# An operand schedule written as a table: the seven-product scheme of an attention, soft-mixture and squared-ReLU kernel

## The chip, the cores and the metric

One core of a Trainium2 chip runs one program. The metric is device time in microseconds (us) of one execution; the profile of one execution and the times of three are shown below. The five engines that compute are called by the names of the profile: PE (matrix products), DVE (VectorE), ACT (ScalarE), POOL (GpSimd); SP issues transfers.

## The reference

Three layers follow each other. Attention over 768 positions with a local window, eight global positions and a linear distance penalty; a soft mixture of experts (every slot a weighted mean of all 3072 tokens, eight small two-layer networks on the slots, every token a weighted mean of the slots); and a last network with squared ReLU. Only the last is touched here:

```python
def _moe2_ref(x, w_in, w_out):
    h = x @ w_in                 # 3072 x 512 times 512 x 2048
    r = np.maximum(h, 0.0)
    g = r * r
    return (g @ w_out).astype(np.float32)
```

Since x itself is a product of token weights (32 slots) and slot outputs, the kernel forms `U = slot_out @ w_in` once and computes `h` as token weights times U, one matmul for 128 columns of `w_in` and 512 tokens.

## The kernel before

**Stages.** From some 225 us on the kernel runs the last network. The 2048 hidden units are cut in five parts q of 256, 384, 384, 512 and 512 (`WIDTHS`), the tokens in six chunks d of 512. For q = 0 to 3 and each d, `gemm1(q, d, j)` makes 128 hidden units: a product h on PE, a ReLU on ACT (line 1049), then `g` as a high part on ACT (1054) and a rest on POOL (1055), for which DVE (1053) or ACT has computed the square in full precision. `gemm2(q, d, m)` multiplies with 128 output columns m: for each j two products with the high part of g (`whi`, `wlo`) and one with its rest, 12 matmuls for four j. An eviction follows: a copy where q = 0 (line 1093, DVE for m = 3 and else ACT), an addition on DVE into `oacc` (1095) for the other q.

**The main loop** (lines 1322 to 1341) takes for each (q, d) four steps m. Below, the steps of q = 3 are numbered k = 4d + m, from 0 to 23. One step advances the generator `background` (the next part's weights: integers are turned into floats on ACT and DVE, U is formed, the weights are split in high part and rest), then issues `gemm1` one chunk ahead, then `gemm2`. At m = 0 only the products with the high part are issued; their rests follow at m = 1. Engines work in the order of issue, each on its own, and wait for each other by semaphores.

**The last part, q = 4,** has 512 units and is computed by a scheme with seven products in place of eight. Units and output columns are halved, and two chunks of tokens (a, b) form a pair p; there are three pairs. The seven left operands are made of weights: blocks x11, x12, x21, x22 and the differences s1 = x21 + x22, s2 = s1 - x11, s4 = x12 - s2, s3 = x11 - x21 (`conv_last`, 983 to 1015). The seven right operands are made of squared-ReLU blocks y11, y12, y22, y21 and t1 = y12 - y11, t2 = y22 - t1, t3 = y22 - y12, t4 = y21 - t2 (`y_make`, 1151 to 1174). Each operand is split in a high part (ACT, 994, 1129, 1131) and a rest, that is operand minus high part (POOL at 996; POOL or DVE at 1132). Two products h (1140) and two ReLUs (1141) and a square (1143) precede each y block. The y blocks and differences share four regions of one buffer: t2 takes y11's place, t3 takes t1's, y21 takes y12's, t4 takes y22's.

`pair` (1176) runs 14 groups g of six matmuls, P1, P5, P6, P3, P7, P2, P4 with two output halves each (lines 1200, 1201, 1203); each group ends with an addition on DVE (1183). After every second group the generator `y_make` is advanced by one operand, which issues all of that operand's operations, from products to rest, in a row. Operands of the next pair begin at g = 6. The first pair's are issued in the last four steps of the main loop.

**Scratch that is shared.** The PSUM tags `h` and `k` have two buffers each; `gemm1` takes them in turn, the products for y always take `h`. The tag `e` (1062, 1136) has two buffers, used by ReLU results of `gemm1` and of y. A buffer is given again only when all who read it are done.

Of the kernel before, what the change touches and what calls it, by code (L numbers as in the profile page):

```python
# [7 lines left out]
F32 = mybir.dt.float32  # L8
# [3 lines left out]
AF = mybir.ActivationFunctionType  # L12
ALU = mybir.AluOpType
# [7 lines left out]
P = 128  # L21
# [9 lines left out]
TB = 256  # L31
WIDTHS = [256, 384, 384, 512, 512]
# [8 lines left out]
def attention_moe_ffn(ctx: ExitStack, tc, qk, vx, nn, phi, w1, w2, w_in, w_out, consts, relw, out):  # L41
# [909 lines left out]
    def conv_in(q):  # L951
        W = WIDTHS[q]
        if q:
            t = slot("p4", [P, 4096], F32, f"winf{q}")
            f = t[:, 0 : 4 * W]
            if q == QL:
                raw["f"] = t[:, 4 * W : 8 * W].rearrange("p (j c) -> p j c", c=DM)
        else:
            f = hZ[:, E * HS : E * HS + 4 * W]
        wq[q] = {"f": f.rearrange("p (a c) -> p a c", c=W)}  # L960
        for c0 in range(0, 4 * W, 512):
            yield from convert(raw[q][0], c0, f[:, c0 : c0 + 512], f"i{q}")
            yield
# [19 lines left out]
    def conv_last():  # L983

        wf = raw["f"]
        for j in range(4):
            yield from convert(raw[QL][1], j * DM, wf[:, j, :], f"o{QL}")
            yield
        t = [slot(tag, [P, 4, 2, 2, 2 * P], F32R, f"x{tag}") for tag in ("s1", "p8")]
        x11, x12, x21, x22 = (wf[:, j : j + 2, c : c + 2 * P] for c, j in ((0, 0), (0, 2), (2 * P, 0), (2 * P, 2)))  # L990

        def operand(n, name, x):
            hi, lo = (t[n // 4][:, n % 4, a] for a in range(2))
            nc.scalar.copy(hi, x)
            yield
            G.tensor_tensor(lo, x, hi.bitcast(F32), op=ALU.subtract)
            xop[name] = hi, lo
            yield

        def diff(name, a, b, op=ALU.subtract):  # L1000
            x = ex.tile([P, 2, 2 * P], F32, tag="cvx", name=name, bufs=2)
            V.tensor_tensor(x, a, b, op=op)  # L1002
            return x

        yield from operand(0, "P1", x11)
        s1 = diff("xs1", x21, x22, ALU.add)
        yield from operand(1, "P5", s1)
        s2 = diff("xs2", s1, x11)
        yield from operand(2, "P6", s2)
        s4 = diff("xs4", x12, s2)  # L1010
        yield from operand(3, "P3", s4)
        s3 = diff("xs3", x11, x21)
        yield from operand(4, "P7", s3)
        yield from operand(5, "P2", x12)
        yield from operand(6, "P4", x22)

    def make_u(q):
        W = WIDTHS[q]
# [66 lines left out]
    def gemm2_lo(pa, q, d, m):  # L1085
        glo, whi = g_of(q, d)[:, 1, :, :], wq[q]["hi"]
        ms = slice(m * P, m * P + P)
        J = WIDTHS[q] // P
        for j in range(J):
            nc.tensor.matmul(pa, lhsT=whi[:, j, ms], rhs=glo[:, j, :], start=False, stop=j == J - 1)  # L1090
        o = oacc[d][:, m, :]
        if q == 0:
            (V.tensor_copy if m == 3 else nc.scalar.copy)(o, pa)
        else:
            V.tensor_tensor(o, pa, o, op=ALU.add)  # L1095

# [26 lines left out]
        t = yt[n - n % 2]  # L1123
        return t[:, n % 2, 0], t[:, n % 2, 1]

    def y_split(name, y, r, eng):
        hi, lo = y_parts(name)
        if r is None:
            nc.scalar.copy(hi, y)  # L1129
        else:  # L1130
            nc.scalar.activation(hi, r, AF.Square)
        eng.tensor_tensor(lo, y, hi.bitcast(F32), op=ALU.subtract)  # L1132
        yop[name] = hi, lo

    def y_block(name, k, half, chunk):
        r = ex.tile([P, 2, 2 * TB], F32, tag="e", name=f"r{name}_{chunk}", bufs=2)
        for jj in range(2):
            j = 2 * half + jj
            ph = fps.tile([P, 2 * TB], F32, tag="h", name=f"h{name}_{chunk}_{jj}", bufs=2)
            nc.tensor.matmul(ph, lhsT=wq[QL]["U"][:, j * P : j * P + P], rhs=cst[:, chunk * 2 * TB : chunk * 2 * TB + 2 * TB], start=True, stop=True)  # L1140
            nc.scalar.activation(r[:, jj], ph, AF.Relu)  # L1141
        y = region(name, k)
        nc.scalar.activation(y, r, AF.Square)  # L1143
        return y, r

    def y_diff(name, k, a, b):
        y = region(name, k)
        V.tensor_tensor(y, a, b, op=ALU.subtract)  # L1148
        return y

    def y_make(p):
        a, b = 2 * p, 2 * p + 1
        y11, r = y_block("y11", 0, 0, a)
        y_split("P1", y11, r, G)
        yield
        y12, _ = y_block("y12", 1, 0, b)
        t1 = y_diff("t1", 2, y12, y11)
        y_split("P5", t1, None, V)
        yield
        y22, r = y_block("y22", 3, 1, b)  # L1160
        t2 = y_diff("t2", 0, y22, t1)
        y_split("P6", t2, None, G)
        yield
        y_split("P3", y22, r, G)
        yield
        t3 = y_diff("t3", 2, y22, y12)
        y_split("P7", t3, None, V)
        yield
        y21, r = y_block("y21", 1, 1, a)
        y_split("P2", y21, r, G)  # L1170
        yield
        t4 = y_diff("t4", 3, y21, t2)
        y_split("P4", t4, None, G)
        yield

    def pair(p, make):
        a, b = 2 * p, 2 * p + 1
        A, Bk = {}, {}

        def add(pa, half, chunk, db, cs, done, eng):  # L1180
            m = 2 * half + db
            o = oacc[chunk][:, m, cs]
            V.tensor_tensor(o, pa[:, cs], o, op=ALU.add)
            if done:
                eng.dma_start(out[m * P : m * P + P, chunk * 2 * TB + cs.start : chunk * 2 * TB + cs.stop], o)

        def group(name, db, cs=slice(0, 2 * TB), n=0):
            if name in ("P1", "P6", "P7", "P4"):
                bank_, key, tag, nb = A, db, "acc", 3
            else:  # L1190
                bank_, key, tag, nb = Bk, (db, name == "P2", n), "k", 2
            new = key not in bank_
            if new:
                bank_[key] = fps.tile([P, 512], F32, tag=tag, name=f"b{p}{name}{db}{n}", bufs=nb)
            pa = bank_[key]
            (whi, wlo), (yhi, ylo) = xop[name], yop[name]
            c = slice(db * P, db * P + P)
            grown = {} if new else {"skip_group_check": True}
            for j in range(2):
                nc.tensor.matmul(pa[:, cs], lhsT=whi[:, j, c], rhs=yhi[:, j, cs], start=new and j == 0, stop=False, **grown)  # L1200
                nc.tensor.matmul(pa[:, cs], lhsT=wlo[:, j, c], rhs=yhi[:, j, cs], start=False, stop=False, **grown)  # L1201
            for j in range(2):
                nc.tensor.matmul(pa[:, cs], lhsT=whi[:, j, c], rhs=ylo[:, j, cs], start=False, stop=j == 1, **grown)
            half, chunk, done = {"P1": (0, a, False), "P5": (1, b, False), "P6": (0, b, False), "P3": (0, b, True),
                                 "P7": (1, b, True), "P2": (0, a, True), "P4": (1, a, True)}[name]
            add(pa, half, chunk, db, cs, done, nc.scalar if n else nc.sync)

        names = [(n, db) for n in ("P1", "P5", "P6", "P3", "P7") for db in range(2)]
        last = p == ND // 2 - 1
        names += [("P2", 0), ("P4", 0), ("P4", 1), ("P2", 1)] if last else [("P2", 0), ("P2", 1), ("P4", 0), ("P4", 1)]  # L1210
        for g, (n, db) in enumerate(names):
            if last and g == len(names) - 1:
                for c in range(2):
                    group(n, db, slice(c * TB, c * TB + TB), c)
            else:
                group(n, db)
            if g % 2 == 0:
                if g == 6:
                    make = y_make(p + 1) if not last else iter(())
                next(make, None)  # L1220
        return make

    def gemm2_first():
        whi, wlo = wq[0]["hi"], wq[0]["lo"]
# [92 lines left out]
            yield from c  # L1317

    ahead = [(q, d) for q in range(QL) for d in range(ND)][1:] + [None]
    make = y_make(0)  # L1320
    first_products = gemm2_first()
    for i in range(QL * ND):
        q, d = i // ND, i % ND
        if d == 0:
            bg = background(q + 1)
            total, room = 5 * (WIDTHS[q + 1] // P) + (17 if q + 1 == QL else 7), 4 * (ND - 1) - 1
        for m in range(4):
            k = 4 * d + m
            for _ in range((k + 1) * total // room - k * total // room):
                next(bg, None)  # L1330
            if d == ND - 1:
                for _ in bg:
                    pass
            if ahead[i]:
                gemm1(*ahead[i], m)
            else:
                next(make)
            if i:
                gemm2(q, d, m)
            else:  # L1340
                next(first_products, None)
    for p in range(ND // 2):
        make = pair(p, make)
    fps.release()
    stream.release()

# [160 lines left out]
```

## Time and profile before

| | us |
|---|---|
| three executions | 522.85, 525.3, 525.71 (median 525.3) |
| the profiled execution, its own time | 523.02 |
| its span (first to last instruction) | 521.2 |
| PE, share of the span with a matmul shown | 97% |
| main loop, q = 3 | some 338 to 446 |
| the three pairs | some 446 to 518 |

The profile lists each instruction with its line, engine, operation, operands and duration. A matmul's end is modelled: matmuls that follow each other are shown overlapping. The idle time in brackets is what the engine stood before that instruction, with the line that released it.

### The profile page before, as it was taken

To read this page: it belongs to the slowest core of one execution; us is meant where nothing else is said; L and a number is where in the kernel's file an instruction comes from. 1 tells how busy PE (TensorE), PEld (TensorE's weight loads), DVE (VectorE), ACT (ScalarE), POOL (GpSimd) and SP (SyncE) were. 2 spreads that over 40 slices of the span, in tenths; PEclk is the share of its full clock that TensorE was granted. 3 is DMA by queue.
4 is the path that set the end of the run, shared out by engine and by line. 5 is a ranking of instruction groups with operands and counts; after the bars stand their busy time and mean duration, and the time that the engine had idled before them with its cause. 6 is when DMAs were issued, how large, how long until landed. Compare 5 with 4: busy or idle time off the path is not lost.

```text
span 521.2 us, 9797 instructions
## 1 busy us (share of the span) xinstructions
PE 504.9 (97%) x3517; PEld 384.2 (74%) x3517; DVE 389.5 (75%) x922; ACT 334.1 (64%) x835; POOL 155.8 (30%) x119
## 2 busy tenths in 40 slices
PE   9999999999999999999999999999999979989897
PEld 6777777677777734588787888788878868768676
DVE  7788878887878747698685738687889853868685
ACT  6977878788788203488865766566646366574740
POOL 7000000000000110001553654476443783546352
PEclk9999999999999999999999999999999999998999
DMA  8789989999994899811312130404000000012224
GB/s 277 254 281 301 374 295 321 334 326 307 309 324 135 292 390 419 347 55 69 121 43 119 21 141 3 161 1 161 1 0 2 0 1 1 1 62 101 84 78 161
DMA packets 25975, 86.93 MB, mean 167 GB/s; under 512 B 2882, under 2 KB 5442, under 8 KB 23746
## 3 DMA queue, kind: packets, MB, share of 16 engines
q1 hardware_dynamic: 25776, 86.13, 46.4%
q8 instruction: 29, 0.48, 0.4%
q14 instruction: 24, 0.20, 0.1%
q10 hardware_dynamic: 146, 0.13, 0.1%
HBM read 79.95 MB, written 6.29 MB: 165 GB/s over the span
## 4 chain that ended last, share of the span: by engine, by line
PE 43%; DVE 11%; ACT 7%; issue 1%; POOL 0%; ACTq 0%; DVEq 0%
PE acc L1081 9%; PE acc L1090 9%; PE acc L1082 9%; PE pSO L923 3%; DVE yt L1148 3%; PE h L1061 2%; ACT yop L1129 1%; ACT ry L1141 1%; DVE yop L1132 1%; ACT yt L1143 1%; DVE xs L1002 1%; PE b2P L1200 1%; DVE oacc_p L1095 1%; PE b2P L1201 1%; ACT rg L1049 1%
## 5 line engine op out<-in xcount | busy, mean ns | idle before, releaser
L1081 PE MATMUL acc<-g,w 128*128 128x512 f32 x280 | 109.5, 391 | 3.8 <-ACT g L1054 2.8
L1082 PE MATMUL acc<-g,w 128*128 128x512 f32 x280 | 109.0, 389 | 0.0
L1055 POOL TENSOR_TENSOR g<-rg,g 128x512 fp32r<-128x512 f32 x60 | 81.3, 1361 | 77.1 <-DVE rg L1053 28.5
L263 ACT ACTIVATE sm<-sm,nm 128x256 f32<-128x256 f32 (+1 forms) x192 | 92.7, 488 | 1.6 <-DVE nm L248 1.6
L1090 PE MATMUL acc<-g,w 128*128 128x512 f32 x280 | 75.8, 390 | 0.0
L248 DVE CUSTOM_DVE_ANT_0 sm<-s,mask 128x256 f32<-128x256 f32 (+1 forms) x192 | 66.8, 397 | 2.0 <-ACT sm L263 1.2
L1049 ACT ACTIVATE rg<-h 128x512 f32<-128x512 f32 (+1 forms) x73 | 43.0, 589 | 38.9 <-PE h L1061 29.2
L1081 PEld LDWEIGHTS acc<-g,w 128*128 128x128 f32 x280 | 52.6, 188 | 16.0 <-ACT g L1054 3.2
L1090 PEld LDWEIGHTS acc<-g,w 128*128 128x128 f32 x280 | 52.5, 188 | 11.3 <-POOL g L1055 0.3
L1082 PEld LDWEIGHTS acc<-g,w 128*128 128x128 f32 x280 | 52.6, 188 | 10.8
L235 PE MATMUL s<-raw 64*128 64x256 f32 (+1 forms) x384 | 52.9, 397 | 0.0
L1132 POOL TENSOR_TENSOR yop<-yt,yop 128x1024 fp32r<-128x1024 f32 x15 | 37.9, 2533 | 42.0 <-ACT yop L1129 20.6
L1095 DVE TENSOR_TENSOR oacc_p<-acc,oacc_p 128x512 f32<-128x512 f32 x48 | 32.4, 687 | 23.3 <-PE acc L1090 23.3
L673 POOL TENSOR_TENSOR lh<-lh 128x256 f32<-128x256 f32 x1 | 0.7, 727 | 158.6 <-PE pt L274 158.6
L274 PE MATMUL pt<-con,sm 128*128 128x128 f32 x352 | 45.7, 278 | 1.6 <-ACT pT L280 1.6
L1054 ACT ACTIVATE g<-rg 128x512 fp32r<-128x512 f32 (+1 forms) x73 | 45.4, 622 | 1.6
L291 PE MATMUL o<-pT,v 128*64 128x128 f32 x704 | 44.2, 276 | 0.0
L274 PEld LDWEIGHTS pt<-con,sm 128*128 128x128 f32 x352 | 38.8, 141 | 7.3 <-ACT pT L280 2.8
L291 PEld LDWEIGHTS o<-pT,v 128*64 128x64 f32 x704 | 37.9, 137 | 6.9 <-ACT sm L263 2.1
L235 PEld LDWEIGHTS s<-raw 64*128 64x128 f32 x384 | 32.2, 194 | 14.6 <-DMA v<-in_vx 6.5
L1053 DVE SCALAR_TENSOR_TENSOR rg<-h,rg 128x512 f32<-128x512 f32 (+1 forms) x49 | 33.0, 675 | 10.0 <-ACT rg L1049 10.0
L263 ACT ACTIVATION_READ_ACCUMULATOR sm<-sm,nm 128x1 f32 x192 | 37.1, 193 | 0.0
(291 smaller groups left out, 874.2 us busy)
## 6 DMA issues: line engine op xcount, KB each, us to landing
w<-in_w SPq DMA_DIRECT2D x40, 512.0 KB, 6.4
raw<-in_qk SPq DMA_DIRECT2D x32, 384.0 KB, 5.0
w<-in_w SPq DMA_DIRECT2D x5, 2048.0 KB, 10.0
v<-in_vx SPq DMA_DIRECT2D x32, 256.0 KB, 4.3
raw<-in_qk SPq DMA_DIRECT2D x16, 320.0 KB, 4.9
win<-in_w_in SPq DMA_DIRECT2D x2, 2048.0 KB, 8.0
wout<-in_w_out SPq DMA_DIRECT2D x2, 2048.0 KB, 8.0
out_x<-oacc_p SPq DMA_DIRECT2D x15, 256.0 KB, 2.1
```

The costliest lines, as they stand in the source:

```text
L235: nc.tensor.matmul(sc[hh][:, tt, 0:n, :], lhsT=r[r0 : r0 + D, tt, :], rhs=rhs, start=True, stop=True)
L248: V.tensor_tensor_reduce(out=sm[:, j, 0:n, :], in0=sc[hh][:, tt, 0:n, :], in1=m[:, 2:3, :] if n == 1 else m[:, 0:2, :], scale=-QK_SCALE, s ...
L263: nc.scalar.activation(sm[:, j, 0:n, :], sm[:, j, 0:n, :], AF.Exp, bias=nm[:, j : j + 1], scale=-1.0, accum_out=chunk_sums(i // NPR)[:, tt ...
L274: nc.tensor.transpose(pp[tt][:, hh, c, :], sm[:, 2 * tt + hh, c, :], ident)
L291: nc.tensor.matmul(o[hh * D : hh * D + D, tt, :], lhsT=v[:, c * 3 if tt == 0 else 1 + c, hh * D : hh * D + D], rhs=pT[:, 2 * tt + hh, c, : ...
L1049: nc.scalar.activation(r, ph, AF.Relu)
L1054: nc.scalar.activation(g2[:, 0, js, cs], r, AF.Square)
L1055: (G if q else V).tensor_tensor(g2[:, 1, js, cs], g, g2[:, 0, js, cs].bitcast(F32), op=ALU.subtract)
L1081: nc.tensor.matmul(pa, lhsT=whi[:, j, ms], rhs=ghi[:, j, :], start=j == 0, stop=False)
L1082: nc.tensor.matmul(pa, lhsT=wlo[:, j, ms], rhs=ghi[:, j, :], start=False, stop=False)
L1090: nc.tensor.matmul(pa, lhsT=whi[:, j, ms], rhs=glo[:, j, :], start=False, stop=j == J - 1)
L1132: eng.tensor_tensor(lo, y, hi.bitcast(F32), op=ALU.subtract)
```

## The change

The generators `operand`, `diff`, `y_split`, `y_block`, `y_diff` and `y_make` go. In their place `y_steps(p)` puts each single operation (products, ReLUs, square, difference, high part, rest) into a numbered slot; slot n >= 0 stands behind group n of its own pair, and slots -14 to -1 stand behind the groups of the pair before (n + 14), or in the last steps of the main loop, two slots to a step, from k = 18. `make(p, slot)` issues what stands in a slot. A rest on POOL is issued as two instructions of half the size. The weight differences get buffers of their own (in the first half of the buffer whose second half holds the weights), all four are issued on DVE at the first two steps of `conv_last`, and `conv_last` takes 8 steps, not 14; it is to be done at k = 17. The eviction for q = 0 is on ACT for every m.

```diff
             if q == QL:
+                raw["s"] = t[:, 0 : 4 * W].rearrange("p (n j c) -> p n j c", n=4, c=2 * P)
                 raw["f"] = t[:, 4 * W : 8 * W].rearrange("p (j c) -> p j c", c=DM)
...
+        s1, s2, s3, s4 = (raw["s"][:, n] for n in range(4))
+        order = [("P1", x11), ("P5", s1), ("P6", s2), ("P3", s4), ("P7", s3), ("P2", x12), ("P4", x22)]
+        diffs = [(s1, x21, x22, ALU.add), (s2, s1, x11, ALU.subtract), (s4, x12, s2, ALU.subtract), (s3, x11, x21, ALU.subtract)]
+        for n in range(len(order) + 1):
+            if n < len(order):
+                name, x = order[n]
+                hi, lo = xop[name] = [t[n // 4][:, n % 4, a] for a in range(2)]
+                nc.scalar.copy(hi, x)
+            for o, x, y, op in diffs[2 * n : 2 * n + 2]:
+                V.tensor_tensor(o, x, y, op=op)
+            if n:
+                name, x = order[n - 1]
+                hi, lo = xop[name]
+                G.tensor_tensor(lo, x, hi.bitcast(F32), op=ALU.subtract)
             yield
...
-            (V.tensor_copy if m == 3 else nc.scalar.copy)(o, pa)
+            nc.scalar.copy(o, pa)
...
+        def low(name, y, eng):
+            hi, lo = y_parts(name)
+            for c in ((0, 1), (1, 2)) if eng is G else ((0, 2),):
+                c = slice(*c)
+                eng.tensor_tensor(lo[:, c], yt[y][:, c], hi[:, c].bitcast(F32), op=ALU.subtract)
+            yop[name] = hi, lo
...
+        for y, half, chunk, slot_ in (("y11", 0, a, -12), ("y12", 0, b, -10), ("y22", 1, b, -8), ("y21", 1, a, -3)):
+            step(slot_, products, y, half, chunk)
+            step(slot_ + 1, relu, y)
+        for y, k, slot_ in (("y11", 0, -10), ("y12", 1, -8), ("y22", 3, -6), ("y21", 1, 0)):
+            step(slot_, square, y, k)
...
+            step(slot_, diff, y, k, x0, x1)
...
+            step(s0, high, name, y)
+            step(s1, low, name, y, eng)
+        return at
...
+    def make(p, slot_):
+        for n in (p, p + 1):
+            if n < ND // 2:
+                for f in plans[n].get(slot_ - (14 if n > p else 0), ()):
+                    f()
...
-            if g % 2 == 0:
-                if g == 6:
-                    make = y_make(p + 1) if not last else iter(())
-                next(make, None)
-        return make
+            make(p, g)
...
-            total, room = 5 * (WIDTHS[q + 1] // P) + (17 if q + 1 == QL else 7), 4 * (ND - 1) - 1
+            total, room = 5 * (WIDTHS[q + 1] // P) + (10 if q + 1 == QL else 7), 4 * (ND - 1) - (2 if q + 1 == QL else 1)
...
             if ahead[i]:
                 gemm1(*ahead[i], m)
-            else:
-                next(make)
+            if q == QL - 1:
+                for slot_ in (2 * k - 48, 2 * k - 47):
+                    if slot_ >= -12:
+                        make(0, slot_)
```

The differences stand in the slots t1 -6, t2 -4, t3 -1, t4 3; high part and rest stand at P1 -9 and -6, P5 -4 and -2, P6 -2 and 0, P3 -1 and 2, P7 1 and 4, P2 2 and 3, P4 4 and 6.

Three places in the order of instructions. **DVE, weight differences (steps 11 to 14 of q = 3; `rg` belongs to `gemm1`, `oacc_p<-acc` is an eviction, `xs` and, in the second fence, `winf<-winf` are the differences).** Before:

```order
L1053 SCALAR_TENSOR_TENSOR rg_3_3_11779<-h_3_3_11777,rg_3_3_11779 128x512
L1095 TENSOR_TENSOR oacc_p_10153<-acc_2_3_11784,oacc_p_10153 128x512
L1002 TENSOR_TENSOR xs_11798<-winf_11480 128x512
L1053 SCALAR_TENSOR_TENSOR rg_4_0_11804<-h_4_0_11802,rg_4_0_11804 128x512
L1002 TENSOR_TENSOR xs_11818<-xs_11798,winf_11480 128x512
L1053 SCALAR_TENSOR_TENSOR rg_4_1_11824<-h_4_1_11822,rg_4_1_11824 128x512
L1095 TENSOR_TENSOR oacc_p_10153<-acc_3_0_11809,oacc_p_10153 128x512
L1095 TENSOR_TENSOR oacc_p_10153<-acc_3_1_11829,oacc_p_10153 128x512
L1002 TENSOR_TENSOR xs_11848<-winf_11480,xs_11818 128x512
L1053 SCALAR_TENSOR_TENSOR rg_4_2_11854<-h_4_2_11852,rg_4_2_11854 128x512
L1095 TENSOR_TENSOR oacc_p_10153<-acc_3_2_11859,oacc_p_10153 128x512
```

With the change:

```order
L937 SCALAR_TENSOR_TENSOR winf_11480<-cvxo_11767,cvyo_11768 128x512
L1045 SCALAR_TENSOR_TENSOR rg_4_0_11796<-h_4_0_11794,rg_4_0_11796 128x512
L1002 TENSOR_TENSOR winf_11480<-winf_11480 128x512 x4
L1045 SCALAR_TENSOR_TENSOR rg_4_1_11821<-h_4_1_11819,rg_4_1_11821 128x512
L1087 TENSOR_TENSOR oacc_p_10153<-acc_3_0_11801,oacc_p_10153 128x512
L1087 TENSOR_TENSOR oacc_p_10153<-acc_3_1_11826,oacc_p_10153 128x512
L1045 SCALAR_TENSOR_TENSOR rg_4_2_11851<-h_4_2_11849,rg_4_2_11851 128x512
```

The four differences, which stood one to a step between gate and eviction, follow each other in one step, ahead of the gate `rg_4_1`.

**PE, step 19 (`h_5_3` is the last product of `gemm1`, `hy` are products for y12).** Before:

```order
L1090 MATMUL acc_4_2_11951<-g_10163,w_11190 128x512 x4
L1061 MATMUL h_5_3_11965<-cu 128x512
L1081 MATMUL acc_4_3_11972<-g_10163,w_11190 128x512
L1082 MATMUL acc_4_3_11972<-g_10163,w_11190 128x512
L1081 MATMUL acc_4_3_11972<-g_10163,w_11190 128x512
```

With the change:

```order
L1082 MATMUL acc_4_2_11954<-g_10163,w_11190 128x512 x4
L1053 MATMUL h_5_3_11968<-cu 128x512
L1132 MATMUL hy_1_0_11976<-cu 128x512
L1132 MATMUL hy_1_1_11978<-cu 128x512
L1073 MATMUL acc_4_3_11986<-g_10163,w_11190 128x512
L1074 MATMUL acc_4_3_11986<-g_10163,w_11190 128x512
```

Two products for y now follow `h_5_3` directly; these three take the PSUM tag `h`, which has two buffers.

**ACT, groups 4 to 8 of the first pair (`ry` are ReLUs of y blocks, `yt<-ry` squares, `yop` high parts; those with 2 and 3 are of the next pair).** Before, from P2's high part on:

```order
L1131 ACTIVATE yop_12088<-ry_0_12107 128x1024
L1129 CAST yop_12133<-yt 128x1024
L1141 ACTIVATE ry_2_12151<-hy_2_0_12152 128x512
L1141 ACTIVATE ry_2_12151<-hy_2_1_12155 128x512
L1143 ACTIVATE yt<-ry_2_12151 128x1024
L1131 ACTIVATE yop_11995<-ry_2_12151 128x1024
L1141 ACTIVATE ry_3_12177<-hy_3_0_12178 128x512
L1141 ACTIVATE ry_3_12177<-hy_3_1_12181 128x512
```

With the change, from P2's high part on:

```order
L1144 ACTIVATE yop_12101<-ry_0_12042 128x1024
L1137 ACTIVATE ry_2_12114<-hy_2_0_12115 128x512
L1137 ACTIVATE ry_2_12114<-hy_2_1_12117 128x512
L1146 CAST yop_12140<-yt 128x1024
L1140 ACTIVATE yt<-ry_2_12114 128x1024
L1137 ACTIVATE ry_3_12142<-hy_3_0_12143 128x512
L1137 ACTIVATE ry_3_12142<-hy_3_1_12145 128x512
L1144 ACTIVATE yop_11984<-ry_2_12114 128x1024
L1140 ACTIVATE yt<-ry_3_12142 128x1024
```

P4's high part (`yop_12140`) and the square of the next pair's y11 now stand behind each other, ahead of the ReLUs of the next pair's y12 (`ry_3_12142`), which empty the PSUM buffers that the products `hy` of y22 take next.

## Rows read from the trace of the kernel before

**Rows 1.** The page, busy us of each engine (share of the span, instructions).
```profile
PE 504.9 (97%) x3517; PEld 384.2 (74%) x3517; DVE 389.5 (75%) x922; ACT 334.1 (64%) x835; POOL 155.8 (30%) x119
```

**Rows 2.** Stretches: length, busy (instructions) of five engines, granted clock, DMA share, GB/s.
```profile
470.00:480.00 10.00, 10.00 (x39) 8.03 (x38) 7.94 (x11) 6.16 (x7) 6.46 (x3) 0.84 0.26 100
480.00:490.00 10.00, 10.00 (x46) 8.13 (x45) 6.16 (x7) 6.07 (x8) 6.48 (x3) 1.00 0.20 79
490.00:500.00 10.00, 7.76 (x27) 5.92 (x26) 7.79 (x10) 5.10 (x6) 3.65 (x2) 0.83 0.35 133
```

**Rows 3.** Timeline, PE: start, us, operation, [shown idle time before, releaser].
```profile
250.89 0.50 PE L1081 MATMUL acc<-g,w 128*128 128x512 f32 x1 [0.57 <-DVE oacc_p L1093]
...
422.99 0.50 PE L1081 MATMUL acc<-g,w 128*128 128x512 f32 x1 [2.75 <-ACT g L1054]
...
425.61 1.98 PE L1090 MATMUL acc<-g,w 128*128 128x512 f32 x8
...
430.37 0.39 PE L1061 MATMUL h<-cu 128*128 128x512 f32 x1
...
443.49 0.50 PE L1081 MATMUL acc<-g,w 128*128 128x512 f32 x1 [0.49 <-DVE oacc_p L1095]
...
468.37 0.50 PE L1200 MATMUL b0P<-yop,xp 128*128 128x512 f32 x1 [1.99 <-DVE oacc L1183]
...
470.42 0.63 PE L1201 MATMUL b1P<-yop,xs 128*128 128x512 f32 x1
470.84 0.63 PE L1200 MATMUL b1P<-yop,xs 128*128 128x512 f32 x1
...
473.53 0.39 PE L1201 MATMUL b1P<-yop,xs 128*128 128x512 f32 x1
...
493.51 0.70 PE L1200 MATMUL b1P<-yop,xp 128*128 128x512 f32 x1 [2.24 <-DVE oacc_p L1183]
...
497.27 0.39 PE L1201 MATMUL b2P<-yop,xs 128*128 128x512 f32 x1
...
505.20 0.50 PE L1200 MATMUL b2P<-yop,xs 128*128 128x512 f32 x1 [1.15 <-DVE oacc_p L1183]
```

**Rows 4.** Timeline, DVE, 408 to 499 us.
```profile
408.54 1.55 DVE L1002 TENSOR_TENSOR xs<-winf 128x512 f32<-128x512 f32 x1
...
411.88 1.17 DVE L1002 TENSOR_TENSOR xs<-xs,winf 128x512 f32<-128x512 f32 x1
...
431.49 0.69 DVE L1053 SCALAR_TENSOR_TENSOR rg<-h,rg 128x512 f32<-128x512 f32 x1 [0.22 <-ACT rg L1049]
...
448.51 1.30 DVE L1148 TENSOR_TENSOR yt<-yt 128x1024 f32<-128x1024 f32 x1
...
463.91 1.47 DVE L1148 TENSOR_TENSOR yt<-yt 128x1024 f32<-128x1024 f32 x1 [3.15 <-ACT yt L1143]
466.49 1.23 DVE L1132 TENSOR_TENSOR yop<-yt,yop 128x1024 fp32r<-128x1024 f32 x1 [1.11 <-ACT yop L1129]
467.63 1.28 DVE L1183 TENSOR_TENSOR oacc<-b0P,oacc 128x512 f32<-128x512 f32 x2
...
477.94 2.47 DVE L1183 TENSOR_TENSOR oacc_p<-b1P,oacc_p 128x512 f32<-128x512 f32 x4
...
498.78 3.42 DVE L1148 TENSOR_TENSOR yt<-yt 128x1024 f32<-128x1024 f32 x1
```

**Rows 5.** Timeline, ACT, 482 to 484 us.
```profile
482.78 1.05 ACT L1129 CAST yop<-yt 128x1024 fp32r<-128x1024 f32 x1 [3.65 <-DVE yt L1148]
483.74 1.07 ACT L1141 ACTIVATE ry<-hy 128x512 f32<-128x512 f32 x2
```

**Rows 6.** Timeline, POOL, 428 to 497 us.
```profile
428.17 2.56 POOL L1055 TENSOR_TENSOR g<-rg,g 128x512 fp32r<-128x512 f32 x2
...
446.33 5.74 POOL L1132 TENSOR_TENSOR yop<-yt,yop 128x1024 fp32r<-128x1024 f32 x2 [6.92 <-ACT yop L1129]
...
496.35 4.76 POOL L1132 TENSOR_TENSOR yop<-yt,yop 128x1024 fp32r<-128x1024 f32 x2 [6.91 <-PE b1P L1203]
```

More of the change, by code (lines that the diff above doesn't have):

```diff
@@ L990, in conv_last @@
         x11, x12, x21, x22 = (wf[:, j : j + 2, c : c + 2 * P] for c, j in ((0, 0), (0, 2), (2 * P, 0), (2 * P, 2)))
-        def operand(n, name, x):
-            hi, lo = (t[n // 4][:, n % 4, a] for a in range(2))
-            nc.scalar.copy(hi, x)
-            yield
[L996 to L1015, printed above, removed]
+        s1, s2, s3, s4 = (raw["s"][:, n] for n in range(4))
[12 more added lines that the diff above has]
+                G.tensor_tensor(lo, x, hi.bitcast(F32), op=ALU.subtract)
+            yield
     def make_u(q):
@@ L1124, in y_parts @@
         return t[:, n % 2, 0], t[:, n % 2, 1]
[L1126 to L1129, printed above, removed]
-        else:
[L1131 to L1151, printed above, removed]
-        a, b = 2 * p, 2 * p + 1
[L1153 to L1174, printed above, removed]
@@ L1177, in pair @@
+    plans = [y_steps(p) for p in range(ND // 2)]
+    def make(p, slot_):
[3 more added lines that the diff above has]
+                    f()
+    def pair(p):
         a, b = 2 * p, 2 * p + 1
@@ L1319, in attention_moe_ffn @@
     ahead = [(q, d) for q in range(QL) for d in range(ND)][1:] + [None]
-    make = y_make(0)
     first_products = gemm2_first()
@@ L1330, in attention_moe_ffn @@
                 next(bg, None)
-            if d == ND - 1:
+            if k == 4 * (ND - 1) - 2:
                 for _ in bg:
@@ L1335, in attention_moe_ffn @@
                 gemm1(*ahead[i], m)
-            else:
-                next(make)
+            if q == QL - 1:
+                for slot_ in (2 * k - 48, 2 * k - 47):
+                    if slot_ >= -12:
+                        make(0, slot_)
             if i:
@@ L1342, in attention_moe_ffn @@
     for p in range(ND // 2):
-        make = pair(p, make)
+        pair(p)
     fps.release()
```

29 lines of the change are left out of this document (28 added, 1 removed).

## The prediction

> **What bounds the kernel now.** The page comes first: PE shows a matmul during 97% of the span [rows 1]. That looks like a full engine, but matmul ends are modelled, so the count of starts decides. The view by stretches shows it for the three pairs: 46 matmuls in the 10 us from 480, but 39 in the stretch from 470, which is busy throughout at a mean granted clock of 0.84, and 27 in the stretch from 490 at 0.83 [rows 2]. So PE is the bound, and what can be won is where it paused or ran slowly.
>
> The timeline of PE gives both. Undisturbed matmuls start 0.227 us apart: eight show 1.98, less the last one's 0.39, over seven steps [rows 3]. The rows with a bracket resume after a pause; since a lone matmul shows 0.39, the loss is the bracket plus 0.16. At 422.99, 443.49, 468.37, 493.51 and 505.20 that is 2.91 + 0.65 + 2.15 + 2.40 + 1.31 = 9.42 us [rows 3]. Behind the pauses of 1.99 and 2.24 us matmuls start up to 0.43 apart (470.42 and 470.84), the half of the pace, 1.2 for 2.4 GHz [rows 3]: from 468.37 to 473.53 fifteen starts took 5.16 us for 3.41, from 493.51 to 497.27 nine took 3.76 for 2.04. That is 3.47 us more. Behind the longest pause, 2.75, the pace stayed full [rows 3]. One pause lies earlier, at 250.89, behind a DVE copy: 0.57 + 0.16 = 0.73.
>
> Why PE pauses is read from DVE's timeline. At 463.91 a difference starts after 3.15 us of waiting for ACT's square, at 466.49 a rest after 1.11 for ACT's high part, and only at 467.63 come two additions, one of which PE awaits [rows 4]. DVE takes its list in order: finished sums stand behind an operand that is made link by link. The pause at 422.99 is the same on ACT, where gates stand behind high parts of weight differences.
>
> **What the change removes.** With each operation two slots behind its input, a link has two groups, 12 x 0.227 = 2.7 us, in which 1.05 us (ACT) or 1.2 to 1.5 us (DVE) of work [rows 4, 5] is done before anybody asks. The four pauses from 443.49 on and the slow pace behind two of them should go. The pause at 422.99 goes because the differences are made before ACT reaches their high parts. The q = 0 copy moves to ACT: its row is the only place where DVE's list holds PE there, so I take the whole 0.73, with the same amount the other way as the other end. All of it is 9.42 + 3.47 + 0.73 = 13.62 us; from the profiled execution's own time, 523.02, this leaves **509.4**, the floor. PE's matmuls are as many as before. Three groups of waits come anew.
>
> **Step 19 of q = 3.** Here `h_5_3` and two products for y12 follow each other into a PSUM tag of two buffers. The third takes the buffer of the first, which ACT and then DVE must have read. At 430.37 such an h starts and DVE's reading begins at 431.49 and takes 0.69 [rows 3, 4]: 1.81 us, where two unhindered starts take 0.45. So at least 1.36 us is lost, where the order before had twelve matmuls of an older chunk in between. It can be more: ACT's ReLU writes into scratch `e`, which POOL must have read for an earlier gate, and POOL's list is denser now. From step 13 to the gate of step 18 it holds twelve instructions (six gates, six rests), at 2.56/2 = 1.28 each [rows 6] 15.4 us. It can begin them when DVE has made the four differences and a gate: differences at 0.6 us (half of a 1024-wide one at 1.2) to 1.36 each (mean of 1.55 and 1.17) [rows 4], with the gate 3.0 to 6.0. POOL is done 18.4 to 21.4 us after step 13's start. PE reaches step 19 after 17 + 13 + 13 + 9 + 17 + 15 = 84 matmuls, 19.1 us. With 1.35 us for ReLU and DVE, the third product starts at 20.9 to 22.8 for an unhindered 19.5. Loss 1.4 to 3.3; nothing in the trace stands at either end, so the middle, **+2.3**.
>
> **The third block of the next pair (pairs 0 and 1).** Behind group 6 PE issues products for y22 into buffers that the ReLUs of y12 must empty. On ACT those stand behind P4's high part and the square of y11, and both wait for t4. t4 stands on DVE behind the addition of group 3: PE gives that group at 26 x 0.227 = 5.9, the addition ends at 6.5 (2.47 for four [rows 4]), t4 at 7.7. The two ACT operations and two ReLUs take 1.05, 1.05 and 1.07 [rows 5]: the first ReLU ends at 10.3, the second at 10.9. PE arrives after 46 matmuls, 10.4. If t4 must let a POOL half (1.28) go first, all comes 1.3 later. Loss 0.2 to 1.5, middle 0.8, twice: **+1.6**.
>
> **POOL and DVE beside each other.** A difference that starts while POOL works takes longer: 3.42 us at 498.78, ending 1.1 us after POOL's two (496.35 + 4.76 = 501.11) [rows 4, 6]; additions out of PSUM keep 0.6. The halves shorten such a wait from some 2.4 to 1.28. For one pair POOL has 10 x 1.28 = 12.8, DVE's six instructions 6 x 1.2 = 7.2, together 20.0 us in which one excludes the other, and PE needs 92 x 0.227 = 20.9. It fits, barely. DVE in all has 14 x 0.62 + 7.2 = 15.9; if each of the six waits a whole half, 23.6, that is 2.7 over PE's need. The rests have four or more groups until they are read, so mean waits should stay hidden: from 0 to 3 x 2.7 = 8.1, I take the smallest pause seen, **+0.7** (443.49), since POOL works 61% of the time and a wait then lasts half of 1.28 on average, a third of the largest. The Trainium skill (SBUF — State Buffer, "Who interferes with whom") says that a VectorE instruction with two SBUF inputs and a GpSimd instruction that reads SBUF exclude each other for the whole instruction. By that rule 20.0 of 20.9 us is real occupancy and the sum stays as it is; by a reading in which the two merely slow each other the 0.7 would vanish. The trace agrees with the rule: the row at 498.78.
>
> The other edits cost nothing: fewer steps of `background` make DVE's conversions slower by a seventh, under PE's full pace; transfers are neither added nor moved past others; additions stay behind their groups, and the last group and its transfer are unchanged.
>
> **Sum:** 509.4 + 2.3 + 1.6 + 0.7 = **514.0**. The three runs reach from 0.2 below to 2.7 above the profiled execution, their median 2.3 above; I leave the number and let the range bear it.
>
> **Rivals.**
>
> A, the new waits hide: POOL runs ahead, t4 gets its turn at once. Then 509.4 + 1.4 + 2 x 0.2 = 511.2, from 509.4 to 511.5. For it: before, POOL stood idle 6.9 us ahead of its rests [rows 6]; against: the least loss at step 19 has no cover. Chance 0.26.
>
> My forecast, 511.5 to 516.5, which also holds a spell at half pace (1.7) behind step 19's pause, as after 493.51: 0.50.
>
> B, DVE becomes the bound: each of its six SBUF instructions waits a POOL half, and additions with sums that PE awaits stand behind. Then 509.4 + 2.3 + 8.1 = 519.8, from 516.5 to 520.4. For it: 20.0 of 20.9 us; against: long due times. 0.17.
>
> C, the change doesn't do what it says: pauses reappear at other places, as at step 19, each with a slow spell, and at least ten of 13.62 us come back: 520.4 to 525.6. 0.04.
>
> D, slower, by the exclusion seen at 498.78. POOL's halves follow each other without letting DVE in between, so each DVE instruction waits for both, 2.56. DVE needs 15.9 + 6 x 2.56 = 31.3 a pair, 10.4 too much, and the time is 509.4 + 2.3 + 31 = 543. It decides from a mean wait of (20.9 + 11.3/3 - 15.9)/6 = 1.5 us, the 11.3 being what is won otherwise. For it: at 498.78 DVE let a whole second instruction pass; against: at 446.33 two POOL instructions took 5.74 instead of 4.76, with the DVE row of 448.51 (1.30) between them [rows 4, 6]. 0.03.
>
> **Numbers.** About 0.5% (2.6 us) is what a measurement of this kernel tells from no change. Faster by more: A, forecast and B, 0.93; same 0.04; slower 0.03. The range goes from A's lower part to within B, with the runs' scatter: 508.8 to 519.5 leaves out the ends of A and B and C and D, under 2 in 10.
>
> **What would show it.** Right: in the profile after, no pause above 1 us between 420 and 425 or inside the groups, except before a product `hy` at step 19 (1.4 to 3.3 us, released by ACT or DVE) and before the third pair of `hy` in pairs 0 and 1 (up to 1.5); 42 or more matmuls in each 10 us; POOL's halves at 1.28; DVE's differences waiting at most 1.3. Wrong: a PE pause in front of a group's third kind of product (a late rest, rival B or D), a clock below 0.95 in the pairs' stretches, or no pause at step 19 (rival A).

## The result, and the profile after

The changed kernel takes **517.06 us**, the median of four runs from 514.59 to 517.64; the kernel before takes 524.43 beside it. The ratio is 0.985, with a 95% interval of 0.981 to 0.989. The profiled execution of the changed kernel took 514.59, against 523.02 before. The forecast, 514.0 with a range of 508.8 to 519.5, was made against the profiled execution and hit it within 0.6 us; the median lies 3.1 above the forecast, inside the range, and that gap has a cause of its own, below.

The page's line of engines, to be held against [rows 1], and the stretches that answer to [rows 2] (length, busy time and instructions of PE, weight loads, DVE, ACT and POOL, granted clock, DMA share, GB/s):

```profile
PE 500.7 (98%) x3517; PEld 381.8 (74%) x3517; DVE 384.9 (75%) x917; ACT 335.4 (65%) x840; POOL 165.6 (32%) x134
```

```profile
422.00:432.00 10.00, 7.31 (x30) 5.34 (x29) 3.97 (x6) 5.41 (x9) 8.46 (x8) 1.00 0.00 0
...
452.00:462.00 10.00, 9.31 (x40) 7.15 (x39) 6.81 (x8) 7.09 (x10) 7.45 (x6) 1.00 0.11 41
...
472.00:482.00 10.00, 9.86 (x43) 7.62 (x42) 7.96 (x11) 9.46 (x13) 9.22 (x6) 1.00 0.10 38
...
492.00:502.00 10.00, 10.00 (x46) 8.29 (x45) 9.74 (x12) 4.01 (x4) 9.24 (x6) 1.00 0.07 27
```

PE has the same 3517 matmuls, so what was won is pauses. Where nothing waits, the pairs now run at 46 matmuls in 10 us, and the clock is at 1.00 in every stretch shown, where [rows 2] had 39 and 27 matmuls at 0.84 and 0.83. Three stretches fall short: 422 to 432, with 30 matmuls and POOL busy for 8.46 of the 10 us, 452 to 462, with 40, and 472 to 482, with 43. The rows of PE's timeline after 400 us which resume behind a pause, with the product that waited ahead of the second one (430.00) and, behind the row ahead of it, a pair of products at 476.03 that shows no bracket:

```profile
415.51 0.50 PE L1073 MATMUL acc<-g,w 128*128 128x512 f32 x1 [1.48 <-DVE oacc_p L1087]
...
429.51 0.50 PE L1053 MATMUL h<-cu 128*128 128x512 f32 x1 [1.70 <-ACT ry L1137]
430.00 0.49 PE L1132 MATMUL hy<-cu 128*128 128x512 f32 x1
431.49 0.50 PE L1132 MATMUL hy<-cu 128*128 128x512 f32 x1 [0.99 <-DVE rg L1045]
...
457.64 0.98 PE L1132 MATMUL hy<-cu 128*128 128x512 f32 x2 [0.69 <-ACT ry L1137]
...
475.27 0.61 PE L1207 MATMUL b1P<-yop,xs 128*128 128x512 f32 x2
476.03 0.98 PE L1132 MATMUL hy<-cu 128*128 128x512 f32 x2
```

All five pauses that the prediction removed are gone, and so is the one at 250.89 [rows 3]. By the prediction's own count (the bracket plus 0.16), three places remain. At step 19: 1.70 + 0.16 + 0.99 + 0.16 = 3.01 us. Before the third pair of `hy` in pair 0: 0.69 + 0.16, and 0.36 more because these two products show 0.98 instead of the 0.61 or 0.62 of any other two in a row, 1.21 together; the same 0.36 stands at 476.03. The third place, at 415.51, nobody had expected: 1.64 us. DVE's timeline ahead of it:

```profile
409.58 4.68 DVE L1002 TENSOR_TENSOR winf<-winf 128x512 f32<-128x512 f32 x4
414.18 0.68 DVE L1045 SCALAR_TENSOR_TENSOR rg<-h,rg 128x512 f32<-128x512 f32 x1
414.78 1.27 DVE L1087 TENSOR_TENSOR oacc_p<-acc,oacc_p 128x512 f32<-128x512 f32 x2
...
430.74 0.69 DVE L1045 SCALAR_TENSOR_TENSOR rg<-h,rg 128x512 f32<-128x512 f32 x1 [2.20 <-ACT rg L1041]
```

The four weight differences, in one piece of 4.68 us, hold a gate and the two additions behind it. PE needs the accumulator that the first addition empties.

The starts of the matmuls show that this count is a little short. Behind a pause the next start comes later than 0.227 us too (0.49 from 429.51 to 430.00), and the pair at 476.03 starts 0.30 later than the two rows of 475.27 would let it, without a bracket. By the starts, step 19 costs 3.49 us (its first undisturbed start comes at 431.83, for 428.34 in an even sequence from 426.75 on), the two places in the pairs 1.22 and 0.67, and 415.51 costs 1.75: 7.1 us in all, for 6.2 by the brackets.

### The profile page after: what moved, and what is told of

Its sections match the earlier page's. It is cut to its first block, busy times and chain, and to the rows that moved or that the text cites. A ratio compares the mean times of both kernels' runs of the same rounds, so it can differ in the third digit from the quotient of the medians.

```text
span 512.8 us, 9826 instructions
## 1 busy us (share of the span) xinstructions
PE 500.7 (98%) x3517; PEld 381.8 (74%) x3517; DVE 384.9 (75%) x917; ACT 335.4 (65%) x840; POOL 165.6 (32%) x134
## 4 chain that ended last, share of the span: by engine, by line
PE 52%; DVE 6%; POOL 2%; issue 1%; ACT 1%; DVEq 0%; ACTq 0%
PE acc L1073 11%; PE acc L1074 11%; PE acc L1082 11%; PE pSO L923 3%; PE h L1053 3%; PE b2P L1207 1%; PE b2P L1205 1%; PE b2P L1204 1%; PE hy L1132 1%; PE b0P L1207 1%; DVE winf L1002 1%; PE b0P L1205 1%; PE b0P L1204 1%; DVE winf L937 1%; DVE rg L1045 1%
## 5 line engine op out<-in xcount | busy, mean ns | idle before, releaser
L1152 POOL TENSOR_TENSOR yop<-yt,yop 128x512 fp32r<-128x512 f32 x30 | 48.2, 1636 | 22.5 <-ACT yop L1146 18.1
```

The source lines that it names most:

```text
L1152: eng.tensor_tensor(lo[:, c], yt[y][:, c], hi[:, c].bitcast(F32), op=ALU.subtract)
```

## The experiments

All ran beside the kernel before, whose medians were 523.41 (eight runs) in the set of 1, 2, 3 and 5, and 524.87 (eleven runs) in that of the others. Each but 6 is an edit of the changed kernel. The changed kernel itself didn't run again in these sets, so a difference of medians to it also holds what separates the sets: the kernel before differed by up to 1.5 us between them (523.41 to 524.87). Profiles differ ahead of the last network too: its first product of `h` starts between 219.8 and 221.0 us in the ten profiles.

**1. Rests on POOL undivided.** Does the cut in halves matter?

```diff
-            for c in ((0, 1), (1, 2)) if eng is G else ((0, 2),):
+            for c in ((0, 2),):
```

> The change with POOL's rests undivided again (one instruction of 1024 columns, not two of 512). Theory (DVE and POOL exclude each other, a half bounds a DVE wait at 1.3 us): DVE's longest difference grows from 2.3 us to 3.4 or more, the pause before the third products for y in pair 0 (0.69 shown) grows to 1 to 2, and pair 1 gets one too: the profiled execution takes 0.5 to 3 us more than the 514.6 of the change. Rival (the halves don't matter, due times are long enough): within 0.5 us of 514.6, the same pauses.

Median 518.00 (517.63 to 521.23), profiled 518.0, 3.4 above the profile of the change. DVE in the second pair:

```profile
467.58 3.38 DVE L1152 TENSOR_TENSOR yop<-yt,yop 128x1024 fp32r<-128x1024 f32 x1
470.89 0.68 DVE L1187 TENSOR_TENSOR oacc<-b0P,oacc 128x512 f32<-128x512 f32 x1
471.50 2.82 DVE L1157 TENSOR_TENSOR yt<-yt 128x1024 f32<-128x1024 f32 x1
474.23 2.47 DVE L1187 TENSOR_TENSOR oacc_p<-b1P,oacc_p 128x512 f32<-128x512 f32 x4
```

And the new pauses on PE in the pairs:

```profile
475.06 0.47 PE L1204 MATMUL b1P<-yop,xs 128*128 128x512 f32 x1 [0.87 <-DVE oacc_p L1187]
...
477.89 0.98 PE L1132 MATMUL hy<-cu 128*128 128x512 f32 x2 [1.21 <-ACT ry L1137]
...
498.82 0.47 PE L1204 MATMUL b2P<-yop,xs 128*128 128x512 f32 x1 [1.32 <-DVE oacc_p L1187]
```

DVE's instructions on SBUF take 3.38 and 2.82 us beside a whole rest on POOL, and the additions that free PE's accumulators come late behind them. That is the mechanism of rivals B and D, switched on by whole rests; the halves keep it off. It cost slightly more than expected.

**2. Weight differences spread over two steps.** Two at step 13, two at step 14, for four in one step.

```diff
-            for o, x, y, op in diffs[2 * n : 2 * n + 2]:
+            for o, x, y, op in diffs[n : n + 1]:
```

> The change with one weight difference issued at each of four steps of the weight generator, not two at each of two. Theory (the new pause of 1.48 us near 415 is an accumulator that DVE frees late, because its additions stand behind four differences of 1.17 us each): that pause goes, and the time falls by 1.6 us to 513.0; step 19 starts no later, so its two pauses stay at 1.7 and 1.0. Rival (POOL's list is full in this stretch, and whatever is won comes back at step 19): the pauses of step 19 grow by about what is won, time within 0.6 us of 514.6.

Median 515.11 (514.86 to 516.91). The pause at 415 is gone. The profiled run, 516.91, shows this instead at step 19:

```profile
429.23 0.50 PE L1053 MATMUL h<-cu 128*128 128x512 f32 x1 [1.94 <-ACT ry L1137]
...
431.20 0.80 PE L1132 MATMUL hy<-cu 128*128 128x512 f32 x1 [0.81 <-DVE rg L1045]
431.80 0.63 PE L1073 MATMUL acc<-g,w 128*128 128x512 f32 x1
432.22 0.63 PE L1074 MATMUL acc<-g,w 128*128 128x512 f32 x1
...
437.29 0.40 PE L1073 MATMUL acc<-g,w 128*128 128x512 f32 x1
```

Of the 1.64 us, 0.24 comes back as a longer first pause there (1.94 for 1.70). How much arrives there is read from the first and the last product of `gemm1` (first and last start at the end of the group's row), the last being step 19's. Here, and then in the change:

```profile
L1053 PE MATMUL h<-cu x70: 389/389/503, 221.1 to 429.2; 128*128 128x512 f32 x70
```

```profile
L1053 PE MATMUL h<-cu x70: 388/389/502, 220.3 to 429.5; 128*128 128x512 f32 x70
```

208.1 us for 209.2, so 1.1 was won: between the theory and its rival. (The rest of the 1.64 is a new small wait at 419.26, 0.15 by its bracket.) Then comes what the profile of the change lacks: starts 0.43 us apart, fourteen in 5.49 us for 14 x 0.227 = 3.18, a loss of 2.31. This is why this run, at a mean clock of 0.993, is no better than the median of the change; the three others, at 0.996, took 514.86 to 515.28.

**3. Step 19 freed.** The first pair's products for y11, y12 and y22 come one step later, and their two PSUM buffers come from two tags in turn.

```diff
-                ph = fps.tile([P, 2 * TB], F32, tag="h", name=f"h{y}_{chunk}_{jj}", bufs=2)
+                ph = fps.tile([P, 2 * TB], F32, tag="hk"[jj] if p == 0 else "h", name=f"h{y}_{chunk}_{jj}", bufs=2)
...
-        for y, half, chunk, slot_ in (("y11", 0, a, -12), ("y12", 0, b, -10), ("y22", 1, b, -8), ("y21", 1, a, -3)):
+        e = 0 if p else 2
+        for y, half, chunk, slot_ in (("y11", 0, a, -12 + e), ("y12", 0, b, -10 + e), ("y22", 1, b, -8 + e), ("y21", 1, a, -3)):
```

(The squares move with them, P1's high part by one slot.)

> The change with the first pair's products for y11, y12 and y22 one step of the main loop later, and the two products of each block in the two PSUM tags h and k in turn, so that none takes a buffer that was written less than a step before. Theory (step 19 loses 1.86 + 1.15 us because its three products share two buffers and wait for ReLUs that wait for POOL): no pause at steps 19 to 21, time 514.6 - 3.0 = 511.6. Rival (POOL is late for the gates in any case): PE waits at steps 20 and 21 for the last gate's high part or rest, 1 to 3 us, time 513 to 515.

Median 511.35 (510.99 to 511.59), ratio 0.977 (0.974 to 0.980). No pause at step 19. The profile's 510.99 is 3.6 under the change's, of which 0.4 lies ahead of the last network (its first product of `h` starts at 219.9 for 220.3); the 3.2 that are left are the 3.49 of step 19 less 0.32, by which the wait in pair 0 is longer. The other places stay:

```profile
415.12 0.50 PE L1073 MATMUL acc<-g,w 128*128 128x512 f32 x1 [1.48 <-DVE oacc_p L1087]
...
454.06 0.98 PE L1132 MATMUL hy<-cu 128*128 128x512 f32 x2 [1.01 <-ACT ry L1137]
```

The median fell by 5.7, more than the profile; about 1 us of that may lie between the sets (the kernel before: 523.41 for 524.43). The runs' clocks are all 0.999 or 1.000 now; those of the change were 0.999, 0.993, 0.996 and 0.993. So what lengthened most of its runs hung on step 19.

**4. Step 19's pause filled.** The wait stays, but PE works through it.

```diff
+            if q == QL - 1 and k == 19:
+                warm(14, con, fps.tile([P, 512], F32, tag="u", name="idle19"))
             if ahead[i]:
                 gemm1(*ahead[i], m)
```

> The change with fourteen small matmuls (256 columns, of constants, into an unused PSUM buffer) ahead of the product of step 19, so that PE works while it waits there. Theory (the runs of the change lie 2 to 3 us above its profile because PE's pause at step 19 is followed by a spell at half pace in most runs): granted clock 0.998 or more in all runs, all within 1 us of 514.6, though nothing of the wait itself is gone. Rival (the spell has nothing to do with the pause): runs at 0.993 to 0.997 and 516 to 518 as for the change.

Four runs from 514.36 to 514.95, median 514.64, at clocks of 1.000; PE at step 19:

```profile
426.68 1.07 PE L1082 MATMUL acc<-g,w 128*128 128x512 f32 x4
427.59 1.70 PE L79 MATMUL idle<-con 128*128 128x256 bf16 x14
429.43 0.50 PE L1053 MATMUL h<-cu 128*128 128x512 f32 x1
...
431.41 0.50 PE L1132 MATMUL hy<-cu 128*128 128x512 f32 x1 [0.99 <-DVE rg L1045]
```

Fourteen idle products fill the first wait, `h_5_3` starts within 0.1 us of where it did, and no useful work comes earlier. Still the median falls by 2.4 us, to the time of the change's best run, although the kernel before was no faster in this set (524.87 for 524.43). So the 2.5 us between profile and median were spells of slow pace, and they follow PE's idleness at step 19. Experiments 3 and 4 show it in two ways, and the profile of experiment 7 caught such a spell.

**5. The table with the old weight operands.** All of the change except the new `conv_last`: its fourteen steps, with a difference ahead of each part, as in the kernel before.

```diff
-        s1, s2, s3, s4 = (raw["s"][:, n] for n in range(4))
...
+        yield from operand(0, "P1", x11)
+        s1 = diff("xs1", x21, x22, ALU.add)
+        yield from operand(1, "P5", s1)
...
-            total, room = 5 * (WIDTHS[q + 1] // P) + (10 if q + 1 == QL else 7), 4 * (ND - 1) - (2 if q + 1 == QL else 1)
+            total, room = 5 * (WIDTHS[q + 1] // P) + (17 if q + 1 == QL else 7), 4 * (ND - 1) - (2 if q + 1 == QL else 1)
```

> The table of slots and the eviction of the change, but the weight operands made as before (difference, high part and rest in turn, 14 steps, the differences in the scratch of two buffers). Theory (the two parts act apart: the weights' part took away 2.9 us at 423 and brought 1.6 at 415): the pause near 420 is back, 2 to 3 us, the one at 415 is absent, 515 to 517 us. Rival (the new order of weights is what gives the table its time): step 19 and the first groups wait for weights, 518 us or more.

Median 512.97 (512.66 to 513.58), ratio 0.980 (0.977 to 0.984), below the 515 to 517 that was expected. No bracket is left at the place of 422.99 [rows 3], step 19 is better than in the change, and a pause stands at a new place, 407.37:

```profile
407.37 0.50 PE L1082 MATMUL acc<-g,w 128*128 128x512 f32 x1 [1.01 <-ACT g L1055]
...
429.60 0.50 PE L1141 MATMUL hy<-cu 128*128 128x512 f32 x1 [0.99 <-DVE rg L1054]
...
455.73 0.99 PE L1141 MATMUL hy<-cu 128*128 128x512 f32 x2 [0.69 <-ACT ry L1146]
```

The pause at 407.37 is of the same kind as that of 422.99, smaller and at another step: 1.17 us for 2.91. ACT's rows ahead of each, in the kernel before and then here (a ReLU stands between the two):

```profile
421.16 0.62 ACT L994 CAST xp<-xs 128x512 fp32r<-128x512 f32 x1 [2.09 <-DVE xs L1002]
...
422.30 0.63 ACT L1054 ACTIVATE g<-rg 128x512 fp32r<-128x512 f32 x1
```

```profile
405.54 0.62 ACT L995 CAST xs<-xs 128x512 fp32r<-128x512 f32 x1 [4.97 <-DVE xs L1003]
...
406.69 0.63 ACT L1055 ACTIVATE g<-rg 128x512 fp32r<-128x512 f32 x1
```

Both times the high part of a weight difference waits for DVE, and the last gate of a chunk (m = 3), which PE needs in the very next step, stands behind it. The table can't be what moved the pause, since it issues nothing before k = 18. Ahead of that, the steps of q = 3 differ from the kernel before in one thing, the pace of the weight generator: `room` stays one step shorter (the last lines of the diff), and each difference is issued a step earlier. The last one so leaves step 15, an m = 3, and the first one comes into step 11, another. This is read from the order of instructions; no run changes the pace alone.

POOL tells why step 19 is better. Here its list ahead of step 19 ends thus:

```profile
424.39 1.30 POOL L997 TENSOR_TENSOR xp<-winf,xp 128x512 fp32r<-128x512 f32 x1
425.65 2.53 POOL L1056 TENSOR_TENSOR g<-rg,g 128x512 fp32r<-128x512 f32 x2
```

And in the change:

```profile
425.04 1.31 POOL L1047 TENSOR_TENSOR g<-rg,g 128x512 fp32r<-128x512 f32 x1
426.29 1.31 POOL L1006 TENSOR_TENSOR xp<-winf,xp 128x512 fp32r<-128x512 f32 x1
427.54 2.52 POOL L1047 TENSOR_TENSOR g<-rg,g 128x512 fp32r<-128x512 f32 x2
```

The old order spreads the seven weight rests from 404.9 to 425.7, while the new one begins them at 411.4, and from 415.0 on POOL has no gap until 430.06. The last two gates end at 428.18 there and at 430.06 here, and the ReLUs that must free the buffer of `h_5_3` wait for the first of them. So, in the company of the table, the weights' new order costs 514.59 - 512.66 = 1.9 us between profiles: 1.64 at 415.51 and 3.01 at step 19 stand against 1.17 and 1.15 here. Between medians it is 4.1, part of which may lie between the sets; the clocks here are 0.999 and 1.000, so the spells are absent behind the shorter pause.

**6. The new weight operands alone,** in the kernel before (the counterpart of 5: `conv_last` and its eight steps, and nothing else).

> The kernel before with the weight operands of the change alone (four differences ahead, eight steps), its y operands made as before. Theory (this part removes the pause of 2.91 at 423 and brings 1.64 near 415, and there is no step 19 with products for y): 523.0 - 2.9 + 1.6 = 521.7, the four pauses of the pairs as before. Rival (the weights' order also shortens the pairs): 519 or less.

Median 520.55 (518.77 to 522.27), ratio 0.993 (0.990 to 0.995), profiled 520.05. The pause at 422.99 is gone and the one at 415 is there; the four pauses from 443.49 on stay, as that of 493.51 does here:

```profile
415.94 0.50 PE L1073 MATMUL acc<-g,w 128*128 128x512 f32 x1 [1.47 <-DVE oacc_p L1087]
...
490.55 0.50 PE L1192 MATMUL b1P<-yop,xp 128*128 128x512 f32 x1 [1.97 <-DVE oacc_p L1175]
```

Alone the part helps, by about 4 us between medians (2.5 to 5 by the interval of the ratio). The profiles differ by 2.97, of which 1.2 lies ahead of the last network (first product of `h` at 219.8 for 221.0), where the edit does nothing. In the pairs one of the two slow spells is absent (granted clock 1.00 from 470 to 475 us, for 0.68 in the kernel before), and a new pause of 1.21 stands at 476.04; so the measured gain isn't only the expected 2.9 less 1.6. The parts don't add: in the company of the table the same new order costs time (experiment 5).

**7. The eviction of q = 0 back on DVE** where m is 3.

```diff
-            nc.scalar.copy(o, pa)
+            (V.tensor_copy if m == 3 else nc.scalar.copy)(o, pa)
```

> The change with the q = 0 copy for m = 3 on DVE again. Theory: the pause of 0.57 near 251 is back and nothing else, 515.3 in a run without a slow spell. Rival (DVE's copy was late only because of other work, and ACT is the tighter engine there): no pause, 514.6 or less.

The pause is back:

```profile
249.77 0.50 PE L1073 MATMUL acc<-g,w 128*128 128x512 f32 x1 [0.56 <-DVE oacc_p L1085]
```

The profiled run, at a mean clock of 0.993, took 517.62 and shows the slow pace behind the change's step 19, with the same first pause:

```profile
429.96 0.50 PE L1053 MATMUL h<-cu 128*128 128x512 f32 x1 [1.70 <-ACT ry L1137]
...
431.94 0.79 PE L1132 MATMUL hy<-cu 128*128 128x512 f32 x1 [0.83 <-DVE rg L1045]
432.53 0.63 PE L1073 MATMUL acc<-g,w 128*128 128x512 f32 x1
432.95 0.63 PE L1074 MATMUL acc<-g,w 128*128 128x512 f32 x1
```

Fourteen starts take 5.51 us from 432.53 on, a loss of 2.33; the change's other runs lie 1.8 to 3.1 above its profile.

The median, 516.60, can't tell 0.7 us. The two runs at a clock of 0.999 took 515.11 and 515.58, against 514.59 for the change at 0.999: the expected size, on few runs.

**8. Three fixes together:** experiments 2 and 3, and y22's products one slot later in pairs 1 and 2, for the 0.69 at 457.64.

```diff
-        for y, half, chunk, slot_ in (("y11", 0, a, -12 + e), ("y12", 0, b, -10 + e), ("y22", 1, b, -8 + e), ("y21", 1, a, -3)):
+        for y, half, chunk, slot_ in (("y11", 0, a, -12 + e), ("y12", 0, b, -10 + e), ("y22", 1, b, -6 if e else -7), ("y21", 1, a, -3)):
```

> The change with the differences spread over two steps, the first pair's blocks one step later in two PSUM tags, and for the later pairs the products for y22 one group later (slot -7 for -8). Theory (the three new waits are separate and each is a buffer that is asked for too soon): no pause over 0.3 us from the main loop to the end, granted clock 0.999 or more in all runs, 511.0 less 1.6 less 1.2 = 508.2. Rival (POOL and DVE, which exclude each other for 20 of 20.9 us a pair, are the next bound): pauses of 0.5 to 2 us inside the pairs, released by DVE or POOL, 509.5 to 512.

Median **508.80** (508.60 to 509.77), ratio 0.970 (0.968 to 0.973), clocks 0.999 to 1.000: faster than both kernels. One bracket is left on PE after 400 us:

```profile
418.78 0.50 PE L1073 MATMUL acc<-g,w 128*128 128x512 f32 x1 [0.16 <-ACT g L1046]
```

```profile
480.00:490.00 10.00, 10.00 (x46) 8.29 (x45) 9.95 (x13) 5.70 (x7) 6.37 (x4) 1.00 0.34 131
```

DVE is busy for 9.95 of 10 us there, and PE doesn't wait for it. A wait without a bracket stays too: the pair of `hy` at 470.29 costs 0.67 by the starts, as at 476.03 in the change. The time lies 0.6 below the prediction's floor of 509.4, which was reckoned as what is left when every pause is gone; 0.4 of that lies ahead of the last network (first product of `h` at 220.6 for 221.0).

## Why the prediction was right, and where it was not

**What the change removes** (13.62) held. None of the five pauses of [rows 3] is left, and the pairs run at full pace. Experiment 6 shows the parts apart: with the new weight operands alone the four pauses from 443.49 on stay, so it is the table that removes them, and the pause at 422.99 goes. The reason given for that one, gates behind high parts of weight differences on ACT, fits: where the old order is kept, in experiment 5, the same chain stops PE at 407.37. The 0.73 of q = 0 is right by its place (experiment 7).

**Step 19** was 2.3 with bounds of 1.4 and 3.3; it measured 3.01 by the brackets, near the upper end. The bounds were reckoned for the start of the third product, and that comes 3.38 late (431.49 for 428.11), just above them. The mechanism is the one described: a PSUM tag of two buffers, and a ReLU that waits through scratch for POOL's gates. Only, POOL's lateness hit one product earlier than I had it, at `h_5_3` (1.70, released by the ReLUs of y11), and the bare chain of ReLU and DVE then came on top (0.99). A denser POOL list was the right reason, but the price was put at step 19 alone. That it makes the weights part a loss beside the table (experiment 5) was not seen.

**The third block** was 1.6 and measured 1.57: 1.21 in pair 0, nothing there in pair 1, and 0.36 at 476.03 (0.67 by the starts), one block earlier than I said. That the total comes out at 1.6 is in part luck.

**POOL and DVE beside each other** was 0.7 and measured nothing. The group of instructions on the y differences, shortest/median/longest in ns:

```profile
L1157 DVE TENSOR_TENSOR yt<-yt x12: 1206/1349/2285, 435.9 to 496.5; 128x1024 f32<-128x1024 f32 x12
```

The longest wait is 2.285 - 1.206 = 1.08 us, less than a POOL half, as rival D's counter-argument had it: POOL lets DVE in between two halves. In experiment 1 the same group reaches 3.31. POOL's halves show 1.30 in the median, as said, and 2.29 at the longest:

```profile
L1152 POOL TENSOR_TENSOR yop<-yt,yop x30: 1290/1298/2285, 435.0 to 502.3; 128x512 fp32r<-128x512 f32 x30
```

The Trainium skill (SBUF — State Buffer, "Who interferes with whom") says that a VectorE instruction with two SBUF inputs and a GpSimd instruction that reads SBUF exclude each other by a lock, which one of them holds for its whole instruction; experiment 1 agrees, with 3.38 us for a rest that takes 1.21 undisturbed, and so do the halves, which cost PE nothing where whole rests did.

**The step that failed is "additions stay behind their groups"**, among the edits that cost nothing. In the main loop that didn't keep them free: the four differences share a step, and two additions stand behind all of them in DVE's list. I had even priced the four, with the gate, at 3.0 to 6.0 us for POOL's sake, and did not ask who else waits behind them on their own engine. It cost 1.64.

The sum by its own terms: 13.62 won, less 3.01, 1.57 and 1.64, is 7.40. The profiles differ by 8.43, of which 0.7 lies before the last network's first product of `h` (221.0 us before, 220.3 after), where the change does nothing; 7.7 is left to compare with 7.40. By the starts, the same places and a short wait at 453.81 held 14.3 us, and the new ones cost 7.1, which leaves 7.2; where the other 0.5 went stays open. The forecast's 9.0 was close in part by luck: a term too many (0.7) and one too few (1.64) stood against each other, and those 0.7 us came on top.

**The number against the median.** "I leave the number and let the range bear it" was the second weak step. I had the slow pace behind two pauses in the trace and gave the chance of another spell at step 19 to the range. Three of four runs of the change lie above 516.7, at clocks of 0.993 to 0.996. Experiment 4 puts that at 2.4 us in the median. A spell of 1.7 was allowed for in the forecast's interval, 511.5 to 516.5, but not in its number, and the median lies above that interval, where only rival B was expected, although B's mechanism is absent.

**The rivals and the signs.** A (no waits) needs experiment 8's edits. The mechanism of B and D shows with whole rests (experiment 1). C did not come about: 3.01 + 1.57 + 1.64 = 6.2 us of pauses stand at new places, 7.1 by the starts, not ten (520.4, where C begins, even stands for eleven). Of the signs in the pairs, 42 matmuls in each 10 us failed once, in the stretch from 452 with 40.

## What to carry to other kernels

When operations move earlier, look on each engine at what then stands behind them: differences taken together to be early held the additions that free PE's accumulator, and rests made denser held a gate. Beside the table, the order that spread them, a difference ahead of each part, was better than the four together; still better was the new order with the differences over two steps and step 19 freed (experiment 8). The old order with step 19 freed wasn't run. Ask, too, which gate is needed first: work that waits does harm ahead of that one (experiment 5). If a pause on PE can't be removed, filling it with idle products can still win back the slow pace that follows it (2.4 us here, experiment 4).

## What the runs showed of the hardware

A pause on PE doesn't always bring the slow pace. Behind 1.70 and 0.99 us at step 19, the profiled run of the change went on at full pace; behind the same 1.70 and then 0.83, the profiled run of experiment 7 did not. The change's other runs, of which no trace was kept, ended 1.8 to 3.1 us later than its profiled one, at a lower mean clock. In experiment 2 the starts were 0.43 us apart for 5.5 us behind 1.94 and 0.81, at a granted clock of one half, 1.2 for 2.4 GHz:

```profile
430.00:435.00 5.00, 4.19 (x10) 3.06 (x10) 0.69 (x1) 4.37 (x7) 1.54 (x2) 0.50 0.02 3
```

With the first of the two waits filled, four runs of four kept the full clock (a mean of 1.000), although 0.99 of waiting was left in the profiled one. What decides between two runs of the same kernel stays open.
